# Loading the last K pair ahead of the last V blocks, and forming most of y as a row of 512 columns

## The chip, the cores and the metric

The kernel runs on one core of one Trainium2 chip. The metric is the device time of one execution in microseconds; lower is better. The engines are called PE (TensorE), DVE (VectorE), ACT (ScalarE), POOL (GpSimd) and SP (SyncE, which issues the large DMA transfers here). The granted clock is the share of its full clock that PE was given. The span is the length of one profiled execution, from its first instruction to its last.

## The reference

Two independent attention blocks, A and B, each decode one token with a cache, and their results stand side by side:

```python
q = (x @ wq).reshape(B, 1, H, Dh)              # x: 1 x 512, H = 32, Dh = 128
scores = einsum("bhqd,bhkd->bhqk", q, k_cache) * Dh ** -0.5   # Sk = 8192
p = softmax(scores)
o = einsum("bhqk,bhkd->bhqd", p, v_cache)
y = o.reshape(1, 1, H * Dh) @ wo               # 4096 x 512
return concatenate([y_A, y_B], axis=-1)        # bf16, 1 x 1 x 1024
```

All data is bf16. Each of the four caches is 64 MiB, so nearly all of the work is reading 285 MB once.

## The kernel before

The heads go two at a time: 32 pairs, 0 to 15 of A and 16 to 31 of B. K or V of one pair is 4 MiB and fills one of five ring slots. Per pair the kernel does this:

- `M`: eight DVE products of K with the query, in place; `fold`: two sets of 16 PE matmuls that add the 128 products of each position up to 8 partial sums; `R`: two DVE reductions that give the scores.
- `m1`, `tr`, `m2`, `bc`: the maximum over all positions (DVE, a transpose on PE, DVE, a broadcast on PE). `exp` on ACT, `sum` on PE, `ri` (reciprocal) on DVE.
- `PV`: 32 matmuls of 512 columns, V as the moving operand; ACT copies the result, `ot` (eight small PE matmuls in the trace) turns it, and `o` on DVE scales it. The last two pairs use `PVs` instead: 128 matmuls with V as the weights and two columns, which give o directly.
- `w`: for the heads whose wo lies in long runs per partition, o is permuted to match (a few tiny PE matmuls, a DVE product, a DVE reduction, and a DVE copy into `sq`).
- `y`: four matmuls per head. `sq` holds o in the diagonal of a 4 x 4 block, so that each of the four 128-column pieces of y comes out in a row of its own.

Every engine does its own list in order; the lists are laid down by this loop. What comes late in the list of an engine waits for all that is ahead of it. In what follows, fold(31,0) and fold(31,1) are the two sets of pair 31, and PV(29) is PV of pair 29.

```python
order = [('wq', a) for a in range(NA)]
for j in range(NPR + 1):
    if j < NPR:
        order.append(('k', j))
    if j == NPR - 1:
        order[-1:] = [('wo', LA), order[-1]]     # wo of B ahead of K31
    if j >= 1:
        order.append(('v', j - 1))
    ...
# so the last loads are: K30, V29, wo, K31 (and wo's last heads), V30, V31 in four parts
...
for j in range(NPR):
    ...                                # M 0 and 1, R(j-1, 1), m1(j-1), ri(j-2), M 2 and 3, tr(j-1)
    if j == NPR - 1:
        for b in wo_early[:1]:
            plan_y(LA, *b)             # heads 0..15 of B
    plan_fold(j, 0)
    if j >= 2:
        plan_ot(j - 2)
    if j == NPR - 1:
        for b in wo_early[1:]:
            plan_y(LA, *b)             # heads 16..23
    ...                                # M 4 to 7, m2, bc, exp of j-1, o(j-2), R(j, 0)
    plan_fold(j, 1)
    if c:
        plan_sum(j - 1)
    if j < NPR - 1:
        if c:
            plan_PV(j - 1)             # PV(29) is the last thing of iteration 30
        ...
        plan_w_ready(j - 2)            # w of heads 16..23 in iteration 29

j = NPR - 1
...                                    # R(31,1), m1, half of PVs(30), tr, w of heads 24..27
for b in perm_l[len(wo_early):]:
    plan_y(LA, *b)                     # heads 24..27
...                                    # bc, exp, other half of PVs(30), sum, o(30), ri
for i, (t0, t1) in enumerate(LAST_PARTS):
    W('PE', *part_of[i])
    plan_PVs(j, t0, t1)
    if i == 0:
        plan_y(LA, *direct_l[0])       # heads 28, 29
plan_o(j)
plan_y(LA, *direct_l[1])               # heads 30, 31
```

## Time and profile before

| | kernel before |
|---|---|
| time, median of the first 3 runs | 681.0 us (680.84 to 683.32) |
| span of the profiled run | 680.3 us |
| bytes moved | 285.6 MB, mean 420 GB/s |
| start of the products of K31 | 646.86 us |
| start of the last output transfer | 678.42 us |

These lines of the page of the kernel before cut the span into 40 equal slices of 17 us. DMA is the busy share of the DMA engines in tenths, GB/s is what the DMA engines moved.

```profile
span 680.3 us, 6183 instructions
...
DMA  9999999999999999999999999999999999999991
GB/s 370 432 432 431 432 431 432 433 430 432 431 432 429 432 434 433 432 431 432 431 430 431 432 433 431 432 431 432 431 429 433 432 432 431 432 431 420 421 423 63
```

The DMA engines are full from the first slice to the last but one, at about 430 GB/s, so 4 MiB takes about 9.75 us. The Trainium skill (DMA: Bandwidth & Descriptors, Where 436 GB/s comes from) gives 435.2 GB/s as the ceiling of the path into SBUF; the stream here agrees with it, at 430 to 432 in each window of 100 us from 100 to 600 us. So no gain is to be expected from a rearrangement in the middle of this kernel. What is open is the end. The windows of the kernel before, with busy us (and number of instructions) per engine, PE's granted clock, the DMA share and the rate:

```profile
core 0: us, PE busy (x) PEld busy (x) DVE busy (x) ACT busy (x) POOL busy (x), PEclk, DMA share, GB/s
660.00:664.00 4.00, 4.00 (x45) 2.32 (x37) 0.80 (x2) 1.14 (x5) 0.00 (x0) 1.00 0.96 392
664.00:668.00 4.00, 3.94 (x81) 2.19 (x71) 1.34 (x5) 0.00 (x0) 0.00 (x0) 1.00 0.47 194
668.00:672.00 4.00, 3.28 (x84) 3.18 (x85) 0.72 (x5) 1.14 (x5) 0.00 (x0) 0.80 0.04 14
```

The stream thins out from 664 and is over by 668. The span ends at 680.3: some 12 us of engine work follow the last bytes. The timeline of the kernel before shows whose work (start, duration, engine, line, operation, output<-inputs, count; in brackets the idle time ahead of it and what ended it). L492 is PV, L579 is DVE's part of w, L387 is M, L171 and L175 are fold, L615 is y.

```profile
615.76 7.07 PE L492 MATMUL otps<-ring,p 128*8 128x512 bf16 x32
...
623.16 0.22 DVE L579 TENSOR_TENSOR wt<-qwps,hmask 128x64 f32<-128x64 f32 x1 [10.32 <-PE qwps L572]
...
623.77 2.35 DVE L387 TENSOR_TENSOR ring<-ring,qbc 128x2048 bf16<-128x2048 bf16 x2
...
639.81 7.07 PE L492 MATMUL otps<-ring,p 128*8 128x512 bf16 x32
646.86 2.36 DVE L387 TENSOR_TENSOR ring<-ring,qbc 128x2048 bf16<-128x2048 bf16 x2 [9.97 <-DMA ring<-in_B_k_cache_dram]
...
650.80 4.91 PE L615 MATMUL yps<-ring,sq 128*4 128x128 bf16 x64
...
655.65 0.39 PE L171 MATMUL fold<-ring,ident 128*128 128x512 bf16 x1
...
662.60 3.40 PE L175 MATMUL fold<-ring,ident 128*128 128x512 bf16 x15
...
677.07 1.01 PE L615 MATMUL yps<-ring,sq 128*4 128x128 bf16 x8 [0.34 <-DVE sq L551]
...
678.42 0.34 SPq L630 DMA_DIRECT2D out_dram<-y_sb  x1
```

Three things are to be seen. DVE stood idle for 9.97 us before the products of K31 at 646.86, waiting for its transfer. PE used that wait: PV(29) ran from 639.81 to 646.88, and the y matmuls of 16 heads (650.80) ran in part under the products. And DVE also waited once on PE: the permutation of heads 16 to 23 stands in PE's list behind PV(28), so DVE stood idle for 10.32 us there and began K30 only at 623.77. Two of the lines of DVE's waits from 560 us on, with the total, the times and the longest, say the same:

```profile
DVE ring L387 <- DMA ring<-in_B_k_cache_dram: 26.3, 4, 10.0
DVE wt L579 <- PE qwps L572: 10.8, 2, 10.3
```

### The profile page before, as it was taken

To read this page: it belongs to the slowest core of one execution; us is meant where nothing else is said; L and a number is where in the kernel's file an instruction comes from. 1 tells how busy PE (TensorE), PEld (TensorE's weight loads), DVE (VectorE), ACT (ScalarE), POOL (GpSimd) and SP (SyncE) were. 2 spreads that over 40 slices of the span, in tenths; PEclk is the share of its full clock that TensorE was granted. 3 is DMA by queue.
4 is the path that set the end of the run, shared out by engine and by line. 5 is a ranking of instruction groups with operands and counts; after the bars stand their busy time and mean duration, and the time that the engine had idled before them with its cause. 6 is when DMAs were issued, how large, how long until landed. Compare 5 with 4: busy or idle time off the path is not lost.

```text
span 680.3 us, 6183 instructions
## 1 busy us (share of the span) xinstructions
PE 561.4 (83%) x3020; PEld 168.8 (25%) x2060; DVE 386.4 (57%) x519; ACT 59.7 (9%) x199; POOL 2.4 (0%) x16
## 2 busy tenths in 40 slices
PE   0477998788799878887998496999789969876978
PEld 0120222122222212222221133232122212222246
DVE  4148656666555566665545626676655376663361
ACT  0020111101110111011101010111011101100000
POOL 1000000000000000000000000000000000000000
PEclk9998999889998988899988797999899979989887
DMA  9999999999999999999999999999999999999991
GB/s 370 432 432 431 432 431 432 433 430 432 431 432 429 432 434 433 432 431 432 431 430 431 432 433 431 432 431 432 431 429 433 432 432 431 432 431 420 421 423 63
DMA packets 11387, 285.61 MB, mean 420 GB/s; under 512 B 1504, under 2 KB 2016, under 8 KB 2400
## 3 DMA queue, kind: packets, MB, share of 16 engines
q1 hardware_dynamic: 11064, 285.22, 97.7%
q8 instruction: 20, 0.33, 0.2%
q10 hardware_dynamic: 296, 0.00, 0.0%
q14 instruction: 7, 0.06, 0.0%
HBM read 285.21 MB, written 0.00 MB: 419 GB/s over the span
## 4 chain that ended last, share of the span: by engine, by line
PE 44%; DMA 43%; DVE 11%; ACT 1%; issue 1%; ACTq 0%; DVEq 0%
DMA ring<-in_B_k_cache_dram 20%; DMA ring<-in_A_k_cache_dram 20%; PE fold L175 18%; PE otps L492 14%; DVE ring L387 8%; DMA xT<-in_B_x_dram 3%; PE qwps L359 3%; PE yps L615 2%; PE stps L532 2%; PE fold L171 2%; DVE s_sb L413 1%; PE otps L514 1%; DVE m L423 1%; ACT qbc L366 1%; PE stps L442 1%
## 5 line engine op out<-in xcount | busy, mean ns | idle before, releaser
L387 DVE TENSOR_TENSOR ring<-ring,qbc 128x2048 bf16<-128x2048 bf16 x256 | 298.3, 1215 | 154.1 <-DMA ring<-in_A_k_cache_dram 89.9
L175 PE MATMUL fold<-ring,ident 128*128 128x512 bf16 x960 | 245.9, 414 | 0.0
L492 PE MATMUL otps<-ring,p 128*8 128x512 bf16 x960 | 212.1, 379 | 0.0
L492 PEld LDWEIGHTS otps<-ring,p 128*8 128x8 bf16 x960 | 81.0, 87 | 116.4
L171 PE MATMUL fold<-ring,ident 128*128 128x512 bf16 x64 | 26.8, 419 | 53.3 <-DVE ring L387 53.3
L532 PEld LDWEIGHTS stps<-ident_f,o 8*128 8x128 f32 x240 | 28.9, 186 | 132.4 <-issue 132.4
L413 DVE TENSOR_REDUCE s_sb<-fold 128x64 f32<-128x512 f32 x64 | 44.0, 687 | 12.9 <-PE fold L175 12.5
L359 PE MATMUL qwps<-ring,xsel 128*128 128x512 bf16 x64 | 18.6, 442 | 29.1 <-DVE xsel L243 24.2
L502 ACT COPY o<-otps 8x512 f32<-8x512 f32 x30 | 17.3, 575 | 284.3 <-PE otps L492 284.3
L463 PEld LDWEIGHTS stps<-rowsum,ones_f 128*128 128x128 f32 x64 | 12.3, 194 | 98.7 <-issue 97.9
L432 PE MATMUL stps<-ident_f,m 128*2 128x128 f32 x32 | 9.2, 286 | 32.4 <-DVE m L423 32.3
L532 PE MATMUL stps<-ident_f,o 8*128 8x2 f32 x240 | 31.5, 249 | 0.0
L448 ACT COPY nb<-stps 128x1 f32<-128x1 f32 x32 | 5.1, 159 | 283.2 <-PE stps L442 283.2
L456 ACT ACTIVATE p<-s_sb,nb 64x128 bf16<-64x128 f32 x64 | 28.0, 437 | 1.9
L551 DVE TENSOR_TENSOR ot<-stps,rinv 128x2 bf16<-128x2 f32 x30 | 4.8, 159 | 40.3 <-PE stps L532 40.0
L171 PEld LDWEIGHTS fold<-ring,ident 128*128 128x128 bf16 x64 | 6.2, 97 | 62.3 <-DVE ring L387 58.2
L579 DVE TENSOR_TENSOR wt<-qwps,hmask 128x512 f32<-128x512 f32 (+3 forms) x5 | 2.2, 441 | 32.0 <-PE qwps L572 31.9
L423 DVE TENSOR_REDUCE m<-s_sb 64x1 f32<-64x128 f32 x64 | 17.9, 280 | 2.1
L615 PE MATMUL yps<-ring,sq 128*4 128x128 bf16 x256 | 17.3, 233 | 1.1 <-DVE sq L593 0.8
L615 PEld LDWEIGHTS yps<-ring,sq 128*4 128x4 bf16 x256 | 16.0, 91 | 1.8 <-issue 1.1
L359 PEld LDWEIGHTS qwps<-ring,xsel 128*128 128x128 bf16 x64 | 6.3, 108 | 40.8 <-issue 28.7
L432 PEld LDWEIGHTS stps<-ident_f,m 128*2 128x2 f32 x32 | 2.6, 80 | 48.6 <-DVE m L423 46.0
(37 smaller groups left out, 98.0 us busy)
## 6 DMA issues: line engine op xcount, KB each, us to landing
ring<-in_A_k_cache_dram SPq DMA_DIRECT2D x16, 4096.0 KB, 34.9
ring<-in_A_v_cache_dram SPq DMA_DIRECT2D x16, 4096.0 KB, 32.4
ring<-in_B_k_cache_dram SPq DMA_DIRECT2D x16, 4096.0 KB, 34.0
ring<-in_B_v_cache_dram SPq DMA_DIRECT2D x15, 4096.0 KB, 32.7
ring<-in_A_wq_dram SPq DMA_DIRECT2D x1, 4096.0 KB, 12.4
ring<-in_B_wq_dram SPq DMA_DIRECT2D x1, 4096.0 KB, 21.8
ring<-in_A_wo_dram SPq DMA_DIRECT2D x1, 4096.0 KB, 36.2
ring<-in_B_wo_dram SPq DMA_DIRECT2D x1, 2048.0 KB, 30.8
```

The costliest lines, as they stand in the source:

```text
L171: return e.matmul(out, lhsT, rhs, start=start, stop=stop)
L175: return e.add_instruction(mybir.InstMatmult(name=nc.get_next_instruction_name(), engine=e.engine, ins=[e.lower_ap(rhs), e.lower_ap(lhsT)] ...
L359: m = e.matmul(qw_ps[:, :].rearrange("p (j d) -> p j d", d=Dh), xsel[:, a, c, par, :], wq[:, c, 4 * g:4 * g + 4, par, :], start=(i == 0), ...
L387: m_val[(j, i)] = INC('DVE', c_m, lambda e: e.tensor_tensor(t, t, qbc[:, a, jj:jj + 1, :].broadcast_to([P, CH, Dh]), ALU.mult))
L413: r_val[(j, h)] = INC('DVE', c_r, lambda e: e.tensor_reduce(s_sb[:, j % 2, h * HT:(h + 1) * HT], fold_ps[h][:, :].rearrange("p (t e) -> p ...
L423: m1_val[j] = INC('DVE', c_m1, lambda e, h=h, q0=q0, q1=q1: e.tensor_reduce(m1[q0:q1, j % 2, h:h + 1], s_sb[q0:q1, j % 2, :], AX.X, ALU.max))
L456: e_val[j] = INC('ACT', c_e, lambda e, h=h, q0=q0, q1=q1: e.activation(p2[q0:q1, j % 2, :, h], s_sb[q0:q1, j % 2, :], AF.Exp, bias=nb[q0:q ...
L463: s_val[j] = INC('PE', c_s, lambda e: e.matmul(st_ps[j % 2][:, P + 2:P + 4], ones_f[:], rowsum[:, j % 2, :], start=True, stop=True))
L492: m = e.matmul(ot_ps[j % 2][0:2 * TB, :], p2[:, j % 2, i:i + TB, :].rearrange("p t h -> p (t h)"), t[:, i:i + TB, :].rearrange("p t d -> p ...
L502: cp_val[j] = INC('ACT', c_cp, lambda e: e.copy(o8[:, j % 2, :], ot_ps[j % 2][0:2 * TB, :]))
L532: m = e.matmul(st_ps[j % 2][:, OC:OC + 2], o8[:, j % 2, i * Dh:(i + 1) * Dh], ident_f[0:2 * TB, 2 * i:2 * i + 2], start=(i == 0), stop=(i ...
L615: m = e.matmul(y_ps[0:NB, 0:P], sq[:, a, h0 + i, b * NB:(b + 1) * NB], wo[:, h0 + i, b, :], start=(first and i == 0 and b == 0), stop=(las ...
```

## The change

The intent: K31 is the start of the longest chain at the end, so load it earlier, ahead of V29, wo and V30. V blocks need only a short chain after landing, and the last heads' block of wo needs the shortest, so it goes last. And y of the other heads is formed as one row (one column of weights, 512 moving columns, one matmul per head in place of four) to shorten it. For B, ACT copies that row out, and four small float32 matmuls with a unit vector (`oneh`) put its four pieces where the remaining heads' small matmuls accumulate.

The core of the diff (cut; declarations and comments left out):

```diff
+        order[-4:] = [order[-4], order[-2], order[-3], ('wo', LA), order[-1], ('v', NPR - 1)]
+        # the last loads: K30, K31, V29, wo, V30, V31, last block of wo
-        wo_early = wo_plan[LA][:sum(b[2] for b in wo_plan[LA]) - 1]
+        wo_early = wo_plan[LA][:-1]
@@ plan_y: one row, of the heads with permuted wo
-                    for b in range(NB):
-                        m = e.matmul(y_ps[0:NB, 0:P], sq[:, a, h0 + i, b * NB:(b + 1) * NB],
-                                     wo[:, h0 + i, b, :], ...)
+                    m = e.matmul(y_ps[0:1, :], w_bf[:, a, h0 + i:h0 + i + 1], wo_of(a)[:, h0 + i, :], ...)
...
+            ve = INC('ACT', c_ye, lambda e: e.copy(y_bulk[:], y_ps[0:1, :]))
+            W('PE', c_ye, ve)
+            def fold_row(e):
+                for b in range(NB):
+                    e.matmul(qw_ps[0:NB, 0:P], oneh[0:1, NB - 1 - b:2 * NB - 1 - b],
+                             y_bulk[0:1, b * P:(b + 1) * P], start=(b == 0), stop=False, ...)
@@ the loop
-            if j == NPR - 1:
-                for b in wo_early[:1]:
-                    plan_y(LA, *b)
-            if j >= 2:
+            if 2 <= j < NPR - 1:
                 plan_ot(j - 2)
-            if j == NPR - 1:
-                for b in wo_early[1:]:
-                    plan_y(LA, *b)
...
+            if c and j < NPR - 2:
+                plan_PV(j - 1)
@@ after the loop
+        plan_PV(j - 2)
+        plan_ot(j - 2)
+        plan_o(j - 2)
         plan_tr(j)
         plan_m2(j)
         plan_bc(j)
         plan_exp(j)
         plan_sum(j)
+        plan_ri(j)
+        plan_w_ready(j - 2)
+        for h0, n, _ in perm_l:
+            plan_y(LA, h0, n)
+        landed('PE', ('v', j - 1))
+        plan_PVs(j - 1, 0, TP)
         plan_o(j - 1)
+        plan_ysq(0)
         for i, (t0, t1) in enumerate(LAST_PARTS):
             W('PE', *part_of[i])
             plan_PVs(j, t0, t1)
         plan_o(j)
-        plan_y(LA, *direct_l[1])
+        plan_ysq(1)
```

The diff moves more than the loads: since V29 now lands after K31, PV(29) goes from the end of iteration 30 to behind fold(31,1), and all of B's y goes behind the last softmax step. PVs(30), which stood in two halves between the short steps of pair 31, goes behind y; its old lines are left out above.

More of the change, by code (lines that the diff above doesn't have):

```diff
@@ L125, in bass_concat_heads__mha_block_cached__gqa_block_cached__decode_kernel @@
         w_bf = ec(nc.sbuf_tensor("w_bf", [P, NA, H], BF16))
-        y_sb = ec(nc.sbuf_tensor("y_sb", [NB, NA, P], BF16))
-        sq = ec(nc.sbuf_tensor("sq", [P, NA, H, NB * NB], BF16))
+        y_row = ec(nc.sbuf_tensor("y_row", [1, NOUT], BF16))
+        y_bulk = ec(nc.sbuf_tensor("y_bulk", [1, NOUT], F32))
+        y_sb = ec(nc.sbuf_tensor("y_sb", [NB, P], BF16))
+        oneh = ec(nc.sbuf_tensor("oneh", [1, 2 * NB - 1], F32))
+        sq = ec(nc.sbuf_tensor("sq", [P, NDIR, NB * NB], BF16))
         fold_ps = [ec(nc.psum_tensor("fold%d" % i, [P, 512], F32)) for i in range(2)]
@@ L195, in bass_concat_heads__mha_block_cached__gqa_block_cached__decode_kernel @@
         INC('DVE', c_init, lambda e: e.memset(sq[:], 0.0))
+        INC('DVE', c_init, lambda e: e.memset(oneh[:], 0.0))
+        W('DVE', c_init, c_init.n)
+        INC('DVE', c_init, lambda e: e.memset(oneh[0:1, NB - 1:NB], 1.0))
         INC('DVE', c_init, lambda e: e.memset(m1[:], -3.0e38))
@@ L260, in bass_concat_heads__mha_block_cached__gqa_block_cached__decode_kernel @@
         order = [('wq', a) for a in range(NA)]
-        for j in range(NPR + 1):
-            if j < NPR:
-                order.append(('k', j))
-            if j == NPR - 1:
-                order[-1:] = [('wo', LA), order[-1]]
+        for j in range(NPR):
+            order.append(('k', j))
             if j >= 1:
                 order.append(('v', j - 1))
-            if j == PPA + 2:
+            if j == min(PPA + 2, NPR - 3):
                 order.append(('wo', 0))
+        order[-4:] = [order[-4], order[-2], order[-3], ('wo', LA), order[-1], ('v', NPR - 1)]
+        assert order[-6:-2] == [('k', NPR - 2), ('k', NPR - 1), ('v', NPR - 3), ('wo', LA)]
         assert order[-1] == ('v', NPR - 1)
@@ L305, in issue @@
             else:
-                early = wo_early if idx == LA else wo_plan[idx]
-                for blk in early:
-                    v = load_wo(idx, s, blk, s_part[4] if idx == LA else s_slot[s])
-                    land_of[('wo', idx, 0)] = (s_part[4] if idx == LA else s_slot[s], v)
-            if (kind, idx) == ('k', NPR - 1):
-                for blk in wo_plan[LA][len(wo_early):]:
-                    v = load_wo(LA, slot_of[('wo', LA)], blk, s_part[5])
-                    land_of[('wo', LA, 1)] = (s_part[5], v)
+                for blk in wo_early if idx == LA else wo_plan[idx]:
+                    land_of[('wo', idx, 0)] = (s_slot[s], load_wo(idx, s, blk, s_slot[s]))
+            if (kind, idx) == ('v', NPR - 1):
+                land_of[('wo', LA, 1)] = (s_part[5], load_wo(
+                    LA, slot_of[('wo', LA)], wo_plan[LA][-1], s_part[5]))
         def load_wo(a, s, blk, ctr):
@@ L548, in plan_o @@
                 src = ot_ps[j % 2][:, 0:2, None].broadcast_to([P, 2, NB])
-                dst = sq[:, a, 2 * jj:2 * jj + 2, 0:NB * NB:NB + 1]
+                i = 2 * (j - NWIDE)
+                dst = sq[:, i:i + 2, 0:NB * NB:NB + 1]
                 rin = rinv[:, j % 2, :, None].broadcast_to([P, 2, NB])
@@ L590, in red @@
                             wt[:, 0:ni * n].rearrange("p (i h) -> p i h", h=n), AX.X, ALU.add)
-                rv = INC('DVE', c_w, red)
-                W('DVE', c_w, rv)
-                w_val[(a, h0)] = INC('DVE', c_w, lambda e, i0=i0: e.tensor_copy(
-                    sq[:, a, h0 + i0:h0 + i0 + ni, 0:NB * NB:NB + 1],
-                    w_bf[:, a, h0 + i0:h0 + i0 + ni, None].broadcast_to([P, ni, NB])))
-        def plan_y(a, h0, n, pm):
-            W('PE', *land_of[('wo', a, int(a == LA and (h0, n, pm) not in wo_early))])
-            if pm:
-                W('PE', c_w, w_val[(a, h0)])
-            else:
-                W('PE', c_o, o_val[a * PPA + (h0 + n) // 2 - 1])
-            first = a not in y_started
-            y_started.add(a)
+                w_val[(a, h0)] = INC('DVE', c_w, red)
@@ L605, in plan_y, with wo_of @@
+        def wo_of(a):
+            return ring[:, slot_of[('wo', a)], 0:H * NOUT].rearrange("p (h n) -> p h n", h=H)
+        def plan_y(a, h0, n):
+            W('PE', *land_of[('wo', a, 0)])
+            W('PE', c_w, w_val[(a, h0)])
+            first = h0 == 0
             if first and a:
                 W('PE', c_ye, a)
-            lastblk = (h0 + n == H)
-            v = c_y.bump() if lastblk else None
+            last = not any(pm and b > h0 for b, _, pm in wo_plan[a])
+            v = c_y.bump() if last else None
@@ L610, in op @@
             def op(e):
-                wo = ring[:, slot_of[('wo', a)], 0:H * NOUT].rearrange(
-                    "p (h b m) -> p h b m", h=H, b=NB)
                 for i in range(n):
-                    for b in range(NB):
-                        m = e.matmul(y_ps[0:NB, 0:P], sq[:, a, h0 + i, b * NB:(b + 1) * NB],
-                                     wo[:, h0 + i, b, :],
-                                     start=(first and i == 0 and b == 0),
-                                     stop=(lastblk and i == n - 1 and b == NB - 1),
-                                     skip_group_check=True)
@@ L620, in op @@
-                if lastblk:
+                    m = e.matmul(y_ps[0:1, :], w_bf[:, a, h0 + i:h0 + i + 1], wo_of(a)[:, h0 + i, :],
+                                 start=(first and i == 0), stop=(last and i == n - 1),
+                                 skip_group_check=True)
+                if last:
                     m.then_inc(c_y.sem, 1)
             OP('PE', op)
-            if lastblk:
+            if not last:
+                return
+            W('ACT', c_y, v)
+            if a != LA:
@@ L624, in plan_y @@
                 release(('wo', a), (c_y, v))
+                ve = INC('ACT', c_ye, lambda e: e.copy(y_row[:], y_ps[0:1, :]))
+                W('ACT', c_ye, ve)
+                s_out.bump(16)
+                OP('ACT', lambda e: e.dma_start(
+                    out[0, 0:1, a * NOUT:(a + 1) * NOUT], y_row[:]).then_inc(s_out.sem, 16))
+                return
+            ve = INC('ACT', c_ye, lambda e: e.copy(y_bulk[:], y_ps[0:1, :]))
+            W('PE', c_ye, ve)
+            if qw_free[0]:
+                W('PE', *qw_free[0])
@@ new lines, in fold_row, with plan_ysq, op @@
+            def fold_row(e):
+                for b in range(NB):
+                    e.matmul(qw_ps[0:NB, 0:P], oneh[0:1, NB - 1 - b:2 * NB - 1 - b],
+                             y_bulk[0:1, b * P:(b + 1) * P], start=(b == 0), stop=False,
+                             skip_group_check=True)
+            OP('PE', fold_row)
+        def plan_ysq(i):
+            h0, n, _ = direct_l[i]
+            last = i == len(direct_l) - 1
+            W('PE', *land_of[('wo', LA, int(last))])
+            W('PE', c_o, o_val[LA * PPA + (h0 + n) // 2 - 1])
+            v = c_y.bump() if last else None
+            def op(e):
+                for k in range(n):
+                    for b in range(NB):
+                        m = e.matmul(qw_ps[0:NB, 0:P], sq[:, 2 * i + k, b * NB:(b + 1) * NB],
+                                     wo_of(LA)[:, h0 + k, b * P:(b + 1) * P],
+                                     start=False, stop=(last and k == n - 1 and b == NB - 1),
+                                     skip_group_check=True)
+                if last:
+                    m.then_inc(c_y.sem, 1)
+            OP('PE', op)
+            if last:
+                release(('wo', LA), (c_y, v))
@@ L625, in plan_y @@
                 W('DVE', c_y, v)
-                ve = INC('DVE', c_ye, lambda e: e.tensor_copy(y_sb[:, a, :], y_ps[0:NB, 0:P]))
-                q = 'SP' if a == LA else 'ACT'
-                W(q, c_ye, ve)
+                ve = INC('DVE', c_ye, lambda e: e.tensor_copy(y_sb[:], qw_ps[0:NB, 0:P]))
+                W('SP', c_ye, ve)
                 s_out.bump(16)
-                OP(q, lambda e: e.dma_start(
-                    out[0, 0, a * NOUT:(a + 1) * NOUT].rearrange("(b m) -> b m", b=NB),
-                    y_sb[:, a, :]).then_inc(s_out.sem, 16))
+                OP('SP', lambda e: e.dma_start(
+                    out[0, 0, LA * NOUT:(LA + 1) * NOUT].rearrange("(b m) -> b m", b=NB),
+                    y_sb[:]).then_inc(s_out.sem, 16))
@@ L662, in bass_concat_heads__mha_block_cached__gqa_block_cached__decode_kernel @@
                 plan_tr(j - 1)
-            if j == NPR - 1:
-                for b in wo_early[:1]:
-                    plan_y(LA, *b)
             plan_fold(j, 0)
-            if j >= 2:
+            if 2 <= j < NPR - 1:
                 plan_ot(j - 2)
-            if j == NPR - 1:
-                for b in wo_early[1:]:
-                    plan_y(LA, *b)
             plan_M(j, 4)
@@ L679, in bass_concat_heads__mha_block_cached__gqa_block_cached__decode_kernel @@
             plan_M(j, 7)
-            if j >= 2:
+            if 2 <= j < NPR - 1:
                 plan_o(j - 2)
@@ L685, in bass_concat_heads__mha_block_cached__gqa_block_cached__decode_kernel @@
                 plan_sum(j - 1)
-            if j < NPR - 1:
-                if c:
-                    plan_PV(j - 1)
-                if j == PPA + 1:
-                    for h0, n, pm in wo_plan[0]:
-                        plan_w(0, h0, n)
-                if j == PPA + 2:
-                    for h0, n, pm in wo_plan[0]:
-                        plan_y(0, h0, n, pm)
+            if c and j < NPR - 2:
+                plan_PV(j - 1)
+            if j == PPA + 1:
+                for h0, n, pm in wo_plan[0]:
+                    plan_w(0, h0, n)
+            if j == PPA + 2:
+                for h0, n, pm in wo_plan[0]:
+                    plan_y(0, h0, n)
+            if j < NPR - 1:
                 plan_w_ready(j - 2)
@@ L700, in bass_concat_heads__mha_block_cached__gqa_block_cached__decode_kernel @@
         plan_m1(j)
-        landed('PE', ('v', j - 1))
-        plan_PVs(j - 1, 0, HT)
+        plan_PV(j - 2)
+        plan_ot(j - 2)
+        plan_o(j - 2)
         plan_tr(j)
-        plan_w_ready(j - 2)
-        assert len(w_done) == len(perm_l)
         plan_m2(j)
-        for b in perm_l[len(wo_early):]:
-            plan_y(LA, *b)
         plan_bc(j)
         plan_exp(j)
-        plan_PVs(j - 1, HT, TP)
         plan_sum(j)
+        plan_ri(j)
+        plan_w_ready(j - 2)
+        assert len(w_done) == len(perm_l) and len(direct_l) == 2
+        for h0, n, _ in perm_l:
+            plan_y(LA, h0, n)
+        landed('PE', ('v', j - 1))
+        plan_PVs(j - 1, 0, TP)
         plan_o(j - 1)
-        plan_ri(j)
-        assert len(direct_l) == 2
+        plan_ysq(0)
         for i, (t0, t1) in enumerate(LAST_PARTS):
@@ L718, in bass_concat_heads__mha_block_cached__gqa_block_cached__decode_kernel @@
             plan_PVs(j, t0, t1)
-            if i == 0:
-                plan_y(LA, *direct_l[0])
         plan_o(j)
-        plan_y(LA, *direct_l[1])
+        plan_ysq(1)
         assert issued[0] == len(queue)
```

## The prediction

> **What bounds the kernel now.** Up to the tail, the DMA stream: the page shows 285.2 MB, DMA share 0.9 or more in every slice but the last, 430 GB/s, so about 9.7 us per 4 MB transfer. Nothing in the change removes bytes. The windows by microsecond show the stream running dry between 664 and 668 us, yet the span is 680.3: some 13 us of engine work follow the last bytes. In the chain of waits that tail hangs on the last K pair (31): it lands at 646.84, DVE had been idle 10.0 us for it, and from there a chain of DVE and PE work, with hardly a gap, takes 33.4 us.
>
> **What the change does there.** K31 is queued two transfers (V29, wo) earlier, so it should land near 628.5 instead of 646.8. That looks like 18 us, but the timeline shows DVE busy with iteration 30 until the reduction that ends near 636.9 (K30 starts at 623.77, itself held by the PE). So iteration 31 starts about 10 us earlier, not 18.
>
> What filled the gap before is moved behind it. The timeline has PV(29) at 639.81 to 646.88 (32 matmuls, 7.07 us) and 96 of the 112 small y matmuls (4.91 and 1.95 us) partly under the wait for the products. All of it now stands, in program order, after fold(31,1), and V30's and V31's products follow all of y.
>
> **The new tail, summed from durations in the timeline of before:**
> - products, fold, reductions of 31 with one half-clock fold (5.0 us, as at 605.8) and one full-clock fold (3.65): fold(31,1) ends near 653.0; sum(30) to 653.2
> - PV(29), 7.0: 660.2
> - ACT copy 0.57, eight transposing matmuls 1.05, o: 662.2
> - transpose, max, broadcast, exp, sum of pair 31, about 2.8: 665.0; last permutation 0.25
> - y row: 28 matmuls of 512 columns. The 512-column PV matmuls run at 0.22 us each: 6.2, plus about 0.8 for a cold clock: 672.3
> - ACT copy of the row 0.6, four float32 matmuls about 1.0 (estimate from the 0.27 us transpose): 674.0
> - PVs(30) 3.6, o 0.3, 8 y matmuls 1.0, PVs(31) 3.6 (1.84 per 64), o 0.3, 8 y matmuls 1.0: 683.9
> - copy 0.3, output DMA 1.95: about 686.2.
>
> The Trainium skill (TensorE: Matmul & The Clock Gate, Part 1) has the PE clock halved after an idle window of about 3.4 us; this trace agrees (granted clock 0.50 from 605.8 to 608, and 0.5 after 671 where only 2-column matmuls ran).
>
> Off the critical path: wo's late block and V31 land near 667, before their readers at about 682; y of the first 32 heads gets cheaper (128 matmuls become 32) inside the DMA-bound middle, worth nothing.
>
> **Prediction.** Span about 686, time 687 us, 0.9% slower; 8 in 10: 683.5 to 691. Faster by over 2%: 0.03; within 2%: 0.93; slower by over 2%: 0.04.
>
> **What would show it.** The DMA stream still ends near 666 to 668; the product of K31 starts near 637, without a DMA wait; PV(29) starts near 653 right behind fold(31,1); the chain of waits from 637 on holds PE and DVE, no DMA; y row takes 6 to 9 us; the last PVs start near 679.
>
> **What would make it wrong.** The DVE starting K31 earlier (then everything shifts by as much); the row matmuls running all at half clock (0.43 each, +5 us) or far faster; the float32 fold costing several us; a hole in the DMA stream from the new slot order (V29 waits for V27's slot, wo for K29's): I see each issue at least 15 us ahead of its turn.

## The result, and the profile after

| | before | after |
|---|---|---|
| time, median of 4 runs | 680.92 us | 688.96 us (687.7 to 691.65) |
| span of the profiled run | 680.3 us | 687.1 us |
| start of the products of K31 | 646.86 us | 637.73 us |
| fold(31,0) starts | 655.65 us | 644.70 us |
| fold(31,1) ends | 666.00 us | 653.88 us |
| last output transfer starts | 678.42 us | 685.16 us |

The ratio is 1.0115 (95% interval 1.0078 to 1.0152): slower by a little over 1%, which is clear of the noise but within 2%.

The same lines of the page after:

```profile
span 687.1 us, 5838 instructions
...
DMA  8999999999999999999999999999999999999970
GB/s 366 445 437 430 426 426 427 434 439 437 425 431 425 431 432 435 430 431 433 428 428 430 435 428 433 434 429 428 435 432 428 431 428 431 432 437 420 427 308 2
```

The stream is as full as before and ends in the 39th slice, so the whole last slice of the span is now without data. Single slices read up to 445 GB/s, above the 435.2 of the page, but each window of 100 us from 100 to 600 us has 430 to 432 here too: a single slice is not that exact. The windows after:

```profile
660.00:664.00 4.00, 2.55 (x16) 1.51 (x14) 0.44 (x2) 0.57 (x1) 0.00 (x0) 1.00 0.96 389
664.00:668.00 4.00, 2.71 (x13) 1.25 (x13) 0.45 (x3) 1.14 (x5) 0.00 (x0) 0.66 0.46 180
668.00:672.00 4.00, 4.00 (x18) 1.51 (x17) 0.00 (x0) 0.00 (x0) 0.00 (x0) 0.91 0.01 4
```

The bytes end at the same time as before, by 668. What follows them has grown from about 12 to about 19 us. The timeline after (L495 is PV, L583 is w, L390 is M, L174 and L178 are fold, L505 and L629 are ACT's copies of PV's result and of the row, L612 is the y row, L636 is its fold, L652 is the small y matmuls):

```profile
616.12 7.07 PE L495 MATMUL otps<-ring,p 128*8 128x512 bf16 x32
...
623.52 0.23 DVE L583 TENSOR_TENSOR wt<-qwps,hmask 128x64 f32<-128x64 f32 x1 [10.32 <-PE qwps L576]
...
623.91 2.35 DVE L390 TENSOR_TENSOR ring<-ring,qbc 128x2048 bf16<-128x2048 bf16 x2
...
637.73 2.35 DVE L390 TENSOR_TENSOR ring<-ring,qbc 128x2048 bf16<-128x2048 bf16 x2
...
644.70 0.56 PE L174 MATMUL fold<-ring,ident 128*128 128x512 bf16 x1 [2.33 <-DVE ring L390]
...
650.48 3.40 PE L178 MATMUL fold<-ring,ident 128*128 128x512 bf16 x15
...
653.92 7.07 PE L495 MATMUL otps<-ring,p 128*8 128x512 bf16 x32
...
661.03 0.57 ACT L505 COPY o<-otps 8x512 f32<-8x512 f32 x1 [9.48 <-PE otps L495]
...
666.05 7.49 PE L612 MATMUL yps<-ring,w_bf 128*1 128x512 bf16 x28
...
673.57 0.57 ACT L629 COPY y_bulk<-yps 1x512 f32<-1x512 f32 x1 [8.20 <-PE yps L612]
...
674.20 1.03 PE L636 MATMUL qwps<-y_bulk,oneh 1*4 1x128 f32 x8 [0.67 <-ACT y_bulk L629]
...
683.80 1.01 PE L652 MATMUL qwps<-ring,sq 128*4 128x128 bf16 x8 [0.43 <-DVE sq L555]
...
685.16 0.34 SPq L665 DMA_DIRECT2D out_dram<-y_sb  x1
```

The products of K31 start at 637.73, right when DVE is done with K30, with no DMA wait ahead of them. What stands ahead has hardly moved: PV(28) starts at 616.12 against 615.76, the products of K30 at 623.91 against 623.77. PV(29), which had run inside a wait, now starts at 653.92 right behind fold(31,1), and the row starts at 666.05. Two of the lines of DVE's waits from 560 us on:

```profile
DVE ring L390 <- DMA ring<-in_B_k_cache_dram: 13.4, 3, 7.7
DVE ot L555 <- PE stps L535: 13.3, 4, 7.4
```

The wait of 10.0 us for the last K is gone from the first line. A wait of 7.4 us of DVE on PE has come in: it is DVE waiting out PV(29). The wait of 10.32 us for the permutation of heads 16 to 23 (623.52) is still there.

The account of the 6.7 us, from the two timelines: the products of K31 start 9.13 us earlier. From there to the start of fold(31,0) it takes 6.97 us in place of 8.79, as no y stands ahead of the fold. The two folds take 9.18 in place of 10.35. From the end of fold(31,1) to the last output transfer it takes 31.28 us in place of 12.42. The sum is -9.13 - 1.82 - 1.17 + 18.86 = +6.74. Of the 18.86, PV(29) with its copy, turning and o is 9.05 (653.92 to the end of o at 662.97), and the row with its copy and fold is 9.1 (666.05 to 675.17) where only 1.05 of y stood before. The rest, about 1.7 by subtraction, fits PE's waits between the short steps of pair 31's softmax (663.1 to 666.0), which PVs(30) had filled before.

### The profile page after: what moved, and what is told of

It reads as the page before. It is cut to its first block, busy times and chain, and to the rows that moved or that the text cites. A ratio compares the mean times of both kernels' runs of the same rounds, so it can differ in the third digit from the quotient of the medians.

```text
span 687.1 us, 5838 instructions
## 1 busy us (share of the span) xinstructions
PE 561.0 (82%) x2848; PEld 159.8 (23%) x1888; DVE 384.9 (56%) x515; ACT 60.8 (9%) x201; POOL 2.4 (0%) x16
## 4 chain that ended last, share of the span: by engine, by line
DMA 44%; PE 42%; DVE 12%; ACT 1%; issue 1%; ACTq 0%; DVEq 0%
DMA ring<-in_A_k_cache_dram 21%; DMA ring<-in_B_k_cache_dram 20%; PE fold L178 17%; PE otps L495 14%; DVE ring L390 9%; DMA xT<-in_B_x_dram 3%; PE qwps L362 2%; PE yps L612 2%; PE stps L535 2%; PE fold L174 2%; DVE s_sb L416 1%; DVE m L426 1%; PE otps L517 1%; ACT qbc L369 1%; PE stps L445 1%
## 5 line engine op out<-in xcount | busy, mean ns | idle before, releaser
L390 DVE TENSOR_TENSOR ring<-ring,qbc 128x2048 bf16<-128x2048 bf16 x256 | 298.3, 1216 | 171.6 <-DMA ring<-in_A_k_cache_dram 93.2
L178 PE MATMUL fold<-ring,ident 128*128 128x512 bf16 x960 | 246.1, 415 | 0.0
L495 PE MATMUL otps<-ring,p 128*8 128x512 bf16 x960 | 212.1, 379 | 0.0
L495 PEld LDWEIGHTS otps<-ring,p 128*8 128x8 bf16 x960 | 81.0, 87 | 116.4
L174 PE MATMUL fold<-ring,ident 128*128 128x512 bf16 x64 | 27.0, 422 | 59.0 <-DVE ring L390 59.0
L505 ACT COPY o<-otps 8x512 f32<-8x512 f32 x30 | 17.2, 574 | 285.0 <-PE otps L495 285.0
L362 PE MATMUL qwps<-ring,xsel 128*128 128x512 bf16 x64 | 16.6, 406 | 28.9 <-DVE xsel L249 24.1
L174 PEld LDWEIGHTS fold<-ring,ident 128*128 128x128 bf16 x64 | 6.2, 97 | 68.5 <-DVE ring L390 64.6
L583 DVE TENSOR_TENSOR wt<-qwps,hmask 128x512 f32<-128x512 f32 (+3 forms) x5 | 2.2, 442 | 31.5 <-PE qwps L576 31.4
L612 PE MATMUL yps<-ring,w_bf 128*1 128x512 bf16 x60 | 14.6, 404 | 0.0
L445 PE MATMUL stps<-m,sel 2*128 2x1 f32 x64 | 11.5, 246 | 0.4 <-DVE m L440 0.4
```

Source lines behind the costliest of these rows:

```text
L174: return e.matmul(out, lhsT, rhs, start=start, stop=stop)
L178: return e.add_instruction(mybir.InstMatmult(name=nc.get_next_instruction_name(), engine=e.engine, ins=[e.lower_ap(rhs), e.lower_ap(lhsT)] ...
L362: m = e.matmul(qw_ps[:, :].rearrange("p (j d) -> p j d", d=Dh), xsel[:, a, c, par, :], wq[:, c, 4 * g:4 * g + 4, par, :], start=(i == 0), ...
L390: m_val[(j, i)] = INC('DVE', c_m, lambda e: e.tensor_tensor(t, t, qbc[:, a, jj:jj + 1, :].broadcast_to([P, CH, Dh]), ALU.mult))
L445: bc_val[j] = INC('PE', c_bc, lambda e: e.matmul(st_ps[j % 2][:, P:P + 1], sel2[:], m2[0:2, j % 2:j % 2 + 1], start=True, stop=True))
L495: m = e.matmul(ot_ps[j % 2][0:2 * TB, :], p2[:, j % 2, i:i + TB, :].rearrange("p t h -> p (t h)"), t[:, i:i + TB, :].rearrange("p t d -> p ...
```

## The experiments

**The theory.** From the products of K30 to the end, the changed kernel is a chain of engine work, with PE as its core. The profile's chain of what ended last shows it. Its last load, with start and duration, is that of K31 in the kernel before, landing at 646.84, and that of K29 in the changed kernel, landing at 599.74:

```profile
615.75 31.09 DMA ring<-in_B_k_cache_dram
...
570.03 29.71 DMA ring<-in_B_k_cache_dram
```

Loading K31 early takes some 9 us of waiting out of the chain. But the work that had filled this wait, and the matmuls under the products, then stand in series behind it, and they are longer than the wait was.

**Rivals.** A: the new load order, or wo as the last transfer, costs by itself. B: K31 early is worth its 9 us with any program. C: the row form of y, with its copy and fold, is what made it slower.

All runs gave the right result. Each was timed in turn with the kernel before on the same chip, and the ratios are to that.

### e1_late_k: the changed kernel, with K31 loaded late again

```diff
-        order[-4:] = [order[-4], order[-2], order[-3], ('wo', LA), order[-1], ('v', NPR - 1)]
+        order[-4:] = [order[-4], order[-3], ('wo', LA), order[-2], order[-1], ('v', NPR - 1)]
```

> The changed kernel, with only the load order put back: K31 again behind V29 and wo; program order, y row and the last wo block stay as changed. Theory (the early K31 is worth its 9 to 10 us, the loss is the engine work now standing behind it): DVE waits for K31 until about 647 instead of starting its products at 637.7, everything behind shifts by that, span about 696, time about 698, ratio to before about 1.024. Rival A (the new load order or wo as the last transfer is what costs): this goes back towards 681 to 683.

Measured: 699.33 us, ratio 1.026 (1.0242 to 1.0277), span 697.9. The products of K31 started at 647.93, after an 8.92 us wait for their transfer. In this program the early K31 is worth about 10 us. The first half of rival A, that the new order of the loads costs, falls.

### e2_early_k_only: the kernel before, with only the loads of the change

(The few lines that keep the y matmuls where they were are left out.)

```diff
-            if j == NPR - 1:
-                order[-1:] = [('wo', LA), order[-1]]
+        order[-5:] = [('k', NPR - 2), ('k', NPR - 1), ('v', NPR - 3), ('wo', LA),
+                      ('v', NPR - 2), ('v', NPR - 1)]
-            if (kind, idx) == ('k', NPR - 1):      # when wo's late block is issued
+            if (kind, idx) == ('v', NPR - 1):
```

> The kernel before, with only the loads of the change (K31 ahead of V29, wo and V30; wo's last block last); its program order and the small y matmuls stay. Theory: the products of K31 start near 637 and are done before they are needed; the PE does PV(29) until 647, waits for wo's blocks until about 648, does the 16-head y (4.9 us) and starts fold(31,0) near 652.5 instead of 655.65; span about 677, time about 678, ratio about 0.995. Rival A (the load order costs): 684 or more. Rival B (early K31 is worth its full 9 us here too): about 671.

Measured: 680.19 us, ratio 0.9983 (0.9968 to 0.9998), span 678.7. Two lines of its timeline, the first products of K31 and y of the first 16 heads:

```profile
636.51 2.35 DVE L389 TENSOR_TENSOR ring<-ring,qbc 128x2048 bf16<-128x2048 bf16 x2
...
648.78 5.36 PE L617 MATMUL yps<-ring,sq 128*4 128x128 bf16 x64 [1.99 <-DMA ring<-in_B_wo_dram]
```

The products start 10 us earlier, yet the span shrinks by 1.6 us only. PE first does PV(29), then stands 1.99 us waiting for wo, then does the y matmuls that stand ahead of fold(31,0) in its list. Rival B falls: an early input is worth only what the list of the next engine lets through. I had expected 677: wo came 0.8 us later than thought (y began at 648.78) and y took 5.36 us rather than 4.9. In this run the last load in that chain is wo's, landing at 648.74, so both PE's list and the later wo hold the gain down.

### e3_no_row: loads and order of the change, y in small matmuls

Edit: the kernel before, with the loads of e2 and the program order of the change; `plan_y` and `sq` as before.

> Loads and program order of the change, but y stays as small matmuls of 4 x 128 columns (no row, no copy of the row, no fold of it). Theory (the order of the work costs, not the row): 112 small matmuls take about 7.2 us where 28 row matmuls took 7.5, and the copy and the fold of the row (1.7 us) go: span about 685, time about 687, ratio about 1.009. Rival C (the row form is what made it slower): 681 or less, ratio 1.000.

Measured: 688.73 us, ratio 1.0107 (1.0087 to 1.0126), span 687.0. This cannot be told from the changed kernel. Its y line:

```profile
665.90 9.21 PE L617 MATMUL yps<-ring,sq 128*4 128x128 bf16 x112
```

The 112 small matmuls took 9.21 us, not the 7.2 expected. The changed kernel's row took 7.49 us, but its copy and fold brought it to 9.1. So the row neither gains nor loses at this place, and rival C falls. The size of my estimate for the small matmuls was wrong.

e3 and e2 have the same loads and the same small matmuls, and differ in the program order alone: 1.0107 against 0.9983, spans of 687.0 and 678.7. So the order of the work costs some 8 us, with nothing else changed.

### e4_pv_early: the changed kernel, with PV(29), ot and o at their old place

```diff
-            if 2 <= j < NPR - 1:
+            if j >= 2:
                 plan_ot(j - 2)
-            if 2 <= j < NPR - 1:
+            if j >= 2:
                 plan_o(j - 2)
-            if c and j < NPR - 2:
+            if c and j < NPR - 1:
                 plan_PV(j - 1)
-        plan_PV(j - 2)
-        plan_ot(j - 2)
-        plan_o(j - 2)
```

> The changed kernel, with PV(29), its transposition and o(29) back at their place in the kernel before: PV(29) at the end of iteration 30, the other two inside iteration 31. Theory: PV(29) runs from about 641 to 648, partly in the PE's wait for the products of K31, fold(31,0) ends near 652 instead of 650 and at full clock, and 7.0 us of PV(29) and 2.1 us of copy, transposition and o leave the end of the chain, 1.0 us comes back in iteration 31: span about 681, time about 682.5, ratio about 1.002. If PV(29)'s place did not matter: 689.

Measured: 684.69 us, ratio 1.0046 (1.0026 to 1.0066). By the ratios (1.0115 and 1.0046) that is 4.7 us less than the changed kernel, uncertain by about 3, where some 6 were expected. The profiled run was the slowest of the four (spans of 681.3 to 684.0); its span of 684.0 is 3.1 us less than that of the changed kernel. PV, the last 15 matmuls of fold(31,0), and the row in its timeline:

```profile
641.77 7.07 PE L495 MATMUL otps<-ring,p 128*8 128x512 bf16 x32
...
649.10 3.40 PE L178 MATMUL fold<-ring,ident 128*128 128x512 bf16 x15
...
661.99 8.30 PE L612 MATMUL yps<-ring,w_bf 128*1 128x512 bf16 x28
```

The direction is as the theory has it. In these two profiled runs more than half of the gain was given back. Fold(31,1) ended 3.4 us later than in the changed kernel (657.26 against 653.88), 1.0 of which was there at the start of K31's products. From there to the row it took 4.73 us in place of 12.17, which is 7.4 less. The row itself took 0.8 more, at a lower clock. What I had missed is that the last reduction and maximum of pair 31 had run hidden under PV(29), and came to light when it moved away.

### e5_wo_not_last: the changed kernel, with wo whole, not last

```diff
-                for blk in wo_early if idx == LA else wo_plan[idx]:
+                for blk in wo_plan[idx]:
                     land_of[('wo', idx, 0)] = (s_slot[s], load_wo(idx, s, blk, s_slot[s]))
-            if (kind, idx) == ('v', NPR - 1):
-                land_of[('wo', LA, 1)] = ...
```

> The changed kernel, with the last wo block loaded together with the rest of wo, ahead of V30 and V31, instead of as the very last transfer. Theory: its reader (the last 8 small matmuls, at 683.8) comes some 16 us after the last bytes, so the time stays that of the changed kernel: ratio 1.0115 plus or minus 0.004. Rival A (wo as the last transfer costs): lower by 0.003 or more.

Measured: 689.83 us, ratio 1.0116 (1.0095 to 1.0137), span 687.1. The time did not move. (In the profiled run K31's products start 1.1 us earlier, at 636.59, and the row takes 1.5 us longer, 8.97.) The place of wo's last block does not matter here, and the second half of rival A falls.

### e6_defer_w and e7_before_defer_w: the same delay of a small step, in both kernels

In e6 the permutation of heads 16 to 23 leaves iteration 29 for the end; in e7, on the kernel before, it leaves it for iteration 30.

```diff
 # e6, on the changed kernel
-            if j < NPR - 1:
+            if j < NPR - 3:
                 plan_w_ready(j - 2)
 # e7, on the kernel before
+                if j != NPR - 3:
+                    plan_w_ready(j - 2)
-                plan_w_ready(j - 2)
```

> The changed kernel; only the permutation of heads 16 to 23 (8 tiny matmuls and two small DVE operations, which in iteration 29 hold DVE back 10.3 us behind PV(28)) is done at the end with that of heads 24 to 27. Theory (the tail from K30 on is a chain of engine work, so a wait at its head counts in full): the products of K30 start at its landing near 619.5 instead of 623.9, and all behind comes about 5 us earlier: span about 682, time about 683.5, ratio about 1.004. If the head of the tail did not matter: 689.

Measured: 684.08 us, ratio 1.0023 (1.0000 to 1.0046), span 684.0. The first products of K30 and of K31 in its timeline:

```profile
619.11 2.36 DVE L390 TENSOR_TENSOR ring<-ring,qbc 128x2048 bf16<-128x2048 bf16 x2 [6.22 <-DMA ring<-in_B_k_cache_dram]
...
632.46 2.35 DVE L390 TENSOR_TENSOR ring<-ring,qbc 128x2048 bf16<-128x2048 bf16 x2
```

> The same delay of the permutation of heads 16 to 23, by one iteration, in the kernel before. Theory: there the last K pair is waited for until 646.8 whatever came earlier, so the products of K30 start 4 to 5 us earlier and DVE then waits that much longer for K31: same time, ratio 1.000 plus or minus 0.003. Rival (it is simply a good edit anywhere): 0.993.

Measured: 682.83 us, ratio 1.0016 (0.9994 to 1.0037), span 683.1. The same two lines:

```profile
619.24 2.36 DVE L387 TENSOR_TENSOR ring<-ring,qbc 128x2048 bf16<-128x2048 bf16 x2 [6.38 <-DMA ring<-in_B_k_cache_dram]
...
647.08 2.36 DVE L387 TENSOR_TENSOR ring<-ring,qbc 128x2048 bf16<-128x2048 bf16 x2 [3.37 <-DMA ring<-in_B_k_cache_dram]
```

The pair tells where each chain begins. In both, K30 starts 4.5 to 4.8 us earlier. In the kernel before, K31 still starts at 647.08, when its transfer lands, and the time does not improve: its last chain begins at a DMA. In the changed kernel, K31 starts 5.3 us earlier (632.46 against 637.73), and by the ratios (1.0115 and 1.0023) the time falls by about 6 us, uncertain by about 3: its last chain runs through the start of K30, and a wait on a small step there now counts. The profiled run of e6 was the slowest of its four (spans of 680.9 to 684.0), and its span is only 3.1 us below that of the changed kernel. The 2.2 us that were lost again in it are, to within 0.2, the permutation itself, now at the end (0.67, from 660.61 to 661.28), and the row, which took 8.88 us there in place of 7.49.

### e8_joined: the findings put together

Edit, on e4: K31 ahead of wo but behind V29; the permutation of heads 16 to 23 deferred; the row's fold split off from `plan_y`; and after the loop:

```diff
+        plan_y(LA, b16[0], b16[1])          # heads 0..15
+        plan_w(LA, b8[0], b8[1])
         plan_tr(j)
+        plan_w(LA, b4[0], b4[1])
         plan_m2(j)
+        plan_y(LA, b8[0], b8[1])            # heads 16..23
         plan_bc(j)
         plan_exp(j)
+        plan_y(LA, b4[0], b4[1])            # heads 24..27, then ACT copies the row
+        landed('PE', ('v', j - 1))
+        plan_PVs(j - 1, 0, TP)
+        plan_o(j - 1)
         plan_sum(j)
         plan_ri(j)
+        plan_fold_row()
+        plan_ysq(0)
```

> The experiments joined: K31 ahead of wo but behind V29, so that PV(29) can fill the PE's wait for the products of K31; PV(29), its transposition and o at their place in the kernel before; the permutation of heads 16 to 23 at the end; the y row in three pieces between the small steps of pair 31, with V30's products ahead of the fold of the row. Theory: fold(31,1) ends near 651, then PE works without a wait of over 0.5 us until V31 is multiplied at about 669.6, only 2 us behind the last bytes: span about 673.5, time about 675, ratio about 0.991, faster than both. If the order on the PE did not matter: no better than 678.

Measured: 678.03 us, ratio 0.9938 (0.9921 to 0.9955), span 676.1. It beats both kernels: the kernel before by 0.6%, and the changed one by about 1.8% (1.0115 over 0.9938, each against the kernel before in its own rounds). PV(29), the first products of K31, the last of fold(31,0), the first piece of the row, and PVs(31):

```profile
634.01 7.07 PE L495 MATMUL otps<-ring,p 128*8 128x512 bf16 x32
638.75 2.36 DVE L390 TENSOR_TENSOR ring<-ring,qbc 128x2048 bf16<-128x2048 bf16 x2 [7.67 <-DMA ring<-in_B_k_cache_dram]
...
645.39 4.60 PE L178 MATMUL fold<-ring,ident 128*128 128x512 bf16 x15
...
654.80 3.61 PE L612 MATMUL yps<-ring,w_bf 128*1 128x512 bf16 x16
...
668.86 3.57 PE L517 MATMUL otps<-p,ring 128*128 128x2 bf16 x128
```

PV(29) now runs while DVE waits for K31, and the row's first 16 heads while DVE reduces. The expected 673.5 was missed by 2.6 us: fold(31,1) ended at 654.75 rather than 651. Of this, 1.4 us are fold(31,0), which ran at half clock after PE's wait for the products (5.0 us from 644.99, against 3.6 in e10 below); the rest was not worked out, but DVE still stood idle for 7.67 us until K31 landed. The fold of the row took 1.86 us at half clock. The mark that I had set for the rival, no better than 678 us, was not beaten as a time: 678.03, in rounds in which the kernel before read 682.33 rather than 680.92. The ratio (0.9938, against 0.9983 for e2) and e10 speak for the order on PE.

### e9_joined_late_k and e10_joined_full_early: the joined kernel with the other two load orders

```diff
 # joined: ... V29, K31, wo, V30, V31
 # e9:  ... V29, wo, K31, V30, V31   (as in the kernel before)
 # e10: ... K31, V29, wo, V30, V31   (as in the change)
```

> The joined kernel with the load order of the kernel before (K31 behind V29 and wo; only wo's last block stays last). Theory (the early K31 is worth its time once the PE's work stands ahead of it): the products of K31 start at about 647 instead of 638.75, fold(31,0) at about 653 instead of 645, all behind comes some 8 us later: span about 684.5, ratio about 1.006. If the program order alone made the gain: 0.994.

Measured: 688.06 us, ratio 1.0082 (1.0052 to 1.0112), span 686.5. K31's products started at 648.38, after DVE had stood idle for 17.08 us. This is 10 us worse than the joined kernel: the early load is what this program lives on.

> The joined kernel with the load order of the change (K31 ahead of V29 too). Theory: PV(29) has to wait for V29 until about 638.5 and runs to 645.6, so fold(31,0) starts near 645.8, warm (3.65 us), and fold(31,1) ends near 654.5, as in the joined kernel: same time, ratio 0.9935 plus or minus 0.003.

Measured: 678.97 us, ratio 0.9946 (0.9917 to 0.9975), span 675.2. The same as the joined kernel, as expected: PV(29) waited 1.79 us for V29 and ran from 638.80, and fold(31,0) then took 3.6 us at full clock from 645.91. e10 has the loads and the row of the changed kernel and differs from it in the program order alone: 0.9946 against 1.0115, spans of 675.2 and 687.1.

## Why the prediction was right

The time forecast was 687.0 us (683.5 to 691); 688.96 was measured, and the span was 687.1 where about 686 was forecast. Point by point:

| step | predicted | measured |
|---|---|---|
| DMA stream ends | 666 to 668 | by 668, as before |
| products of K31 start | near 637, no DMA wait | 637.73, none |
| fold(31,1) ends | near 653.0 | 653.88 |
| PV(29) with copy, ot, o ends | 662.2 | 662.97 |
| row starts, and takes | 665.25; 6.2 and about 0.8 | 666.05; 7.49 |
| copy and fold of the row end | 674.0 | 675.2 |
| output transfer starts | about 684.2 | 685.16 |

The deciding step was that DVE is not free for K31 when it lands, but at about 637: so the load gains 9 us, not the 18 of its earlier place in the queue. e1 puts a number on this, about 10 us. The second was that PV(29) and y are not new work but moved work, out of a wait and into a series; the pairs e2 and e3, and e10 and the changed kernel, which differ in program order alone, show that it is the order that costs (spans of 678.7 and 687.0, 675.2 and 687.1), and e4 shows the part of PV(29). That the row is no gain follows from e3. That wo's place is off the critical path is shown by e5.

Three sizes were off, and small. The chain ran about 0.9 us late by fold(31,1), as fold(31,0) took 5.3 us from 644.70 rather than 5.0, and K31's products started 0.7 late, as fold(30,0) took 5.8 us from 630.14 where it had taken 5.0 in the kernel before. The time of a run is 1.8 us above its profiled span (688.91 against 687.1), and I had taken about 1. And I called the row "cheaper" for A's 32 heads in the middle: 128 small matmuls took 7.31 us there (from 406.93 in the kernel before), 32 of 512 columns took 7.07 (from 405.74 in the changed one), so they are hardly cheaper for PE; it was rightly taken as worth nothing, as the stream is the limit there. That the sum met the profiled span to within 1 us is in part luck: the spans of the four runs lie between 686.0 and 689.9.

The clock was cited rightly for the fold at 605.8 (PE had been busy for only 0.27 us from 602 to 605.8) and then allowed for as a sum of 0.8 us. The Trainium skill (TensorE: Matmul & The Clock Gate, Part 1) says that the window by which the clock is set is free-running and the number of slow matmuls varies from run to run. The runs fit this: the same 28 matmuls took 7.49 us in the changed kernel, 7.89 in e1, 8.30 in e4, 8.88 in e6 and 8.97 in e5, where the granted clock was 0.50 from 664 to 668. Differences of 1.5 us between such tails are therefore not to be laid to the edit.

What stays open: why the steps before iteration 30 drift by about 1 us between kernels that are the same up to there (K30's products began at 623.77, 623.91 and 625.00 in three of them) was not looked into.

## What to carry to other kernels

An input that comes earlier is worth only the time until the next engine in the chain is free, and what had been filling the old wait must find another place; find that place before moving the load. Count the tail as one list per engine, in order, with measured durations: here this gave the end of a sequence of nearly 50 us to within 1 us in the profiled run. The same small wait can be free in one version and cost its length in the next, so after a chain's head has moved, look again at the waits that were harmless.

## What the Trainium skill lacked or had wrong

- TensorE: Matmul & The Clock Gate, Part 1, ties the half clock to windows in which PE is idle. Here the clock also falls while PE is busy all the time with matmuls of two columns: in the joined kernel PE was busy 1.00 of each us from 664 to 667, in PVs(30) and what follows, and the granted clock went from 0.94 to 0.50, as this line of its windows shows for 665 to 666 (busy as the profile has it, where the ends of matmuls are modelled):

```profile
665.00:666.00 1.00, 1.00 (x31) 1.00 (x28) 0.13 (x1) 0.00 (x0) 0.00 (x0) 0.50 0.56 228
```

  The kernel before shows the same: PE busy for 4.00 us of 4.00 from 670 to 674, at a clock of 0.55. The two-column matmuls themselves hardly lose by it (128 of them took 3.37 us in the changed kernel, at clock 1.00 for the most part, and 3.57 at 0.50), but the wider ones behind them do: the fold of the row took 1.03 us in the changed kernel and 1.86 in the joined one.
- DMA: Bandwidth & Descriptors gives rates for whole transfers, and nothing on how a long stream ends. Here the DMA share falls to 0.47 in the window of 664 to 668 of the kernel before, and from 664 to 667 of the joined kernel to 0.56 or 0.57 of each us: the last 3 us of this stream run at about half rate. The last transfers are small here (V31 comes as 2048, 1024, 512 and 512 KB), and whether that is the reason was not tested. It is not wo's last block: with it moved forward in e5, the share from 664 to 668 was 0.45. The share is a mean over the 16 engines, so that some of them are done before the others would fit, but no view that I used shows the engines one by one.
- TensorE: Matmul & The Clock Gate, Part 2, Back-to-back issue gap, gives for a stream of weight load and matmul pairs "N=128 → ~81 ns/MM" and "N=512 → ~131 ns/MM", and calls N / 2.4 + 2.5 ns the gap of an isolated one. Here the pairs in the middle of the kernel, with weights of 4 columns and of 1, took 57 ns each at 128 columns (7.31 us for 128) and 221 ns at 512 (7.07 us for 32), and PV, with weights of 8 columns, also 221 ns (7.07 us for 32). That is near the page's formula for the isolated gap (56 and 216) and not near its figures for the stream. The narrow weights could account for the first difference, but not for the second, where the runs are slower than the page. It is also why the row gained so little: four matmuls of 128 columns stream as long as one of 512.
